# A dense MLP in chunks of 436, 436, 312, 496 and 496 tokens, its pair sums made in place, the pair's norm started beside the third chunk's, and its reciprocal deviation kept in PSUM

## The chip, the cores and the metric

The kernel runs on one core of one Trainium2 chip. The metric is device time of one execution in microseconds (us). The core has a matrix engine (TensorE, PE), a vector engine (VectorE, DVE), an activation engine (ScalarE, ACT), GpSimd (POOL) and a queue engine (SyncE, SP) that issues most DMAs. Each engine runs its own list of instructions in order; semaphores tie the lists together. TensorE writes its products to PSUM, eight banks of 512 fp32 columns; everything else lives in SBUF.

## What is computed

Three layers follow each other: a windowed attention, a gated convolution MLP, and a Fourier mixing with a dense MLP. The change touches the last part alone, with 4 × 544 = 2176 tokens of 512 features:

```python
u = x + mixed
mu = np.mean(u, axis=-1, keepdims=True)
var = np.mean((u - mu) ** 2, axis=-1, keepdims=True)
un = (u - mu) / np.sqrt(var + 1e-06)
ch = np.maximum(un @ w_ch1, 0.0) @ w_ch2     # 512 -> 2048 -> 512
return (u + ch).astype(np.float32)
```

## The kernel before

Features lie on the partitions and tokens along the columns, so a matmul takes a 128 × 128 block of weights and the columns of one chunk of tokens. Each fp32 product is made of three matmuls on high and low parts (`mm3`, L172).

The tokens of the dense MLP are cut into five chunks (`WIDE`, L40). Chunks 0, 1 and 2 go the plain way: `ln(c)` makes the norm in nine steps, `c_g1` (L1002) makes a block of 128 hidden features with 12 matmuls and turns it into a high and a low part `hd` (one ACT and one DVE instruction), and `c_g2` (L1026) adds the block to four accumulators with 12 matmuls. A list of 48 pairs of chunk and block sets the order. In slot v of this list TensorE gets `c_g1(v)` and then `c_g2(v-2)`, 24 matmuls; slots 32 to 47 are those of chunk 2. Blocks alternate between two PSUM banks, so `c_g1(v)` waits until `hd` of block v-2 has been read out of its bank.

Chunks 3 and 4 are a pair: their first layer is made by a scheme of Strassen's kind (`pair`, L1182). Eight rounds q of 7 products, of 6 matmuls each, give four blocks of hidden features; eight plain products would need 48. The second layer is plain, 24 matmuls per round and 192 behind the rounds. Each product lands in one of four banks in turn and is added to sums by DVE (`p1`, `u2`, `w5`, `c21`, `late`). The weights of a round come by DMA: `aw` (L1069) into a buffer of the pool `up`, and two sums of weights `mag` from `sval` in DRAM, which `s_make` (L1052) has computed and stored earlier (slots 17 to 31).

`pair_norm` (L1127) normalises the pair before: per half `x_sum` (L1079), `x_center` (L1093), `x_square` (L1099) and `x_scale` (L1108). A sum over the features is two matmuls with `ones` on a high and low part `sr` (`x_mean`, L1087); they stand in TensorE's list between the slots. Then `t_split` makes the operands of the seven products.

The program fixes the order of TensorE and SP as written; those of DVE, ACT and POOL come from a list scheduler with priorities. `step(lnq)` (L1270) runs one step of the front generator per slot, so `pair_norm`, put into the queue at slot 32, begins when `ln(2)` is through, at slot 36.

The pool `up` has three buffers. Through the last third they hold `cf`, a scratch tile (`cft[0]`), the tokens `uc` of a chunk, and `xsr` and later `aw`:

```python
up = ctx.enter_context(tc.tile_pool(name="up", bufs=3))          # L250
cft.append(up.tile([128, 5, NT], F32, tag="u", name="cf"))       # L957
t = up.tile([128, 3, 512], F32R, tag="u", name="aw")             # L1069
```

Of the kernel before, what the change touches and what calls it, by code (L numbers as in the profile page):

```python
# [12 lines left out]
F32 = mybir.dt.float32  # L13
F32R = mybir.dt.float32r
# [22 lines left out]
KEPT = [0, 16, 1, 17, 2, 18, 3, 19, 4, 5, 6, 7]  # L37
TAIL = [x for m in range(8, 16) for x in (m, 16 + m)]
NT = 436
WIDE = [436, 436, 436, 434, 434]  # L40
NPB, NHB = 3, 3
MT = [(0, 92), (92, 92), (184, 90)]
PLAN = """
# [109 lines left out]
def fused_kernel(ctx: ExitStack, tc: tile.TileContext, d, out):  # L153
# [29 lines left out]
    def f32(ap):  # L183
        return ap.bitcast(F32)
# [750 lines left out]

    ln_t, uc_t, rs_t, cft = {}, {}, {}, []

    def width(c):
        return WIDE[c]

    def load_uc(c, dst=None):
        if dst is None:
            uc_t[c] = up.tile([128, 5, NT], F32, tag="u", name="uc")
            dst = uc_t[c][:, 0:4]
        a0 = a = sum(WIDE[:c])
        z = a0 + width(c)
# [55 lines left out]
    def c_g1(v):  # L1002
        if not 0 <= v < len(plan):
            return
        c, m = plan[v]
        ch, cl = ln_t[c]
        n = width(c)
        o = bank("g1" if m % 2 else "pv")[:, 0:n]
        w = ch1[m]
        for k in range(4):  # L1010
            f = slice(128 * k, 128 * k + 128)
            mm3(o, w[:, 0, f], w[:, 1, f], ch[:, k], cl[:, k], k == 0, k == 3)
        hd = lw.tile([128, 2, NT], F32R, tag="hd", name="hd", bufs=3)[:, :, 0:n]
# [12 lines left out]
    def c_g2(v):  # L1026
        if not 0 <= v < len(plan):
            return
        c, m = plan[v]
        n = width(c)  # L1030
        if m == 0 or c < 2 and m == 8:
            for e in range(4):
                acc[e] = bank(f"a{e}")[:, 0:n]
        for e in range(4):
            c_mm(v, e)
        if m == 15 or c < 2 and m == 7:
            uc = uc_t[c]
            tmp = cft[0][:, 0:4, 0:n]
            for e in range(4):
                dve.tensor_mul(tmp[:, e], acc[e], rs_t[c])  # L1040
            for e in range(4):
                o = uc[:, e, 0:n]
                dve.tensor_add(o, o, tmp[:, e])
                if m == 15:
                    sp.dma_start(out[128 * e:128 * e + 128, NT * c:NT * c + n], o)

    NW = WIDE[3]
    T_SLOTS = []
    T_ORDER = ("b11", "b21", "t2", "t1", "t3", "b22", "t4")
    sval, two, t_hl, s_hl, a_hl = {}, {}, {}, {}, {}  # L1050
# [26 lines left out]
            s_hl[q] = [put(wp, f"w{k}", mags[k]) for k in range(2)]  # L1077

    def x_sum(j):  # L1079
        cf = cft[0]  # L1080
        x, sr = two["x"][j], two["sr"]
        dve.tensor_add(cf[:, 0:2, 0:NW], x[:, 0:2], x[:, 2:4])
        dve.tensor_add(cf[:, 0, 0:NW], cf[:, 0, 0:NW], cf[:, 1, 0:NW])
        act.copy(sr[:, 0], cf[:, 0, 0:NW])
        dve.tensor_sub(sr[:, 1], cf[:, 0, 0:NW], f32(sr[:, 0]))

    def x_mean(o):  # L1087
        sr = two["sr"]
# [8 lines left out]
            dve.tensor_sub(x, x, mu[:, None, :].to_broadcast([128, 2, NW]))  # L1097

    def x_square(j):  # L1099
        cf, sr = cft[0], two["sr"]  # L1100
        for k in (slice(0, 2), slice(2, 4)):
            act.activation(cf[:, k, 0:NW], two["x"][j][:, k], AF.Square)
        dve.tensor_add(cf[:, 0:2, 0:NW], cf[:, 0:2, 0:NW], cf[:, 2:4, 0:NW])
        dve.tensor_add(cf[:, 0, 0:NW], cf[:, 0, 0:NW], cf[:, 1, 0:NW])
        act.copy(sr[:, 0], cf[:, 0, 0:NW])
        dve.tensor_sub(sr[:, 1], cf[:, 0, 0:NW], f32(sr[:, 0]))

    def x_scale(j):  # L1108
        va = x_mean(fbank()[:, 0:NW])
        rs = cft[0][:, 4, 0:NW]  # L1110
        act.activation(rs, va, AF.Sqrt, bias=eps)
        dve.reciprocal(rs, rs)
        for k in (slice(0, 2), slice(2, 4)):
            x = two["x"][j][:, k]
            dve.tensor_mul(x, x, rs[:, None, :].to_broadcast([128, 2, NW]))
# [55 lines left out]
    four = itertools.cycle(("s", "t", "g1", "pv"))  # L1171

    def new_hd():
        return lw.tile([128, 2, NT], F32R, tag="hd", name="hd", bufs=3)[:, :, 0:NW]

    def out_add(c, e, o, a=0, z=NW):
        u = uc_t[c][:, e, a:z]
# [2 lines left out]
        sp.dma_start(out[128 * e:128 * e + 128, t0 + a:t0 + z], u)  # L1180

    def pair():  # L1182
        hbig = [xp.tile([128, 10, NT], F32, tag="x", name="hh") for _ in range(2)]
        block = [hbig[k // 10][:, k % 10, 0:NW] for k in range(20)]
        p1, u2, w5, c21 = block[0:4]
        late = {m: block[4 + k] for k, m in enumerate(x for q in range(8) for x in (q, q + 8))}
        accs = [bank(f"a{e}")[:, 0:NW] for e in range(4)]
        hds = {}

# [12 lines left out]
        for q in range(8):  # L1202
            s_load(q + 1)
            aw, (s24, s13) = a_hl.pop(q), s_hl.pop(q)
            wa = {"a11": aw[:, 0:2, 0:256], "a12": aw[:, 0:2, 256:512], "a22": aw[:, 2].rearrange("p (a b) -> p a b", a=2)}
            for s_, nm in ((s24, "s2 s4"), (s13, "s3 s1")):
                for k, n_ in enumerate(nm.split()):
                    wa[n_] = s_[:, :, 256 * k:256 * k + 256]

            def prod(w, x):  # L1210
                o = bank(next(four))[:, 0:NW]
                for k in range(2):
                    f = slice(128 * k, 128 * k + 128)
                    mm3(o, wa[w][:, 0, f], wa[w][:, 1, f], t_hl[x][k][:, 0], t_hl[x][k][:, 1], k == 0, k == 1)
                return o

            x = prod("a11", "b11")
            with pri("cev"):
                act.copy(p1, x)
            if q:  # L1220
                g2(accs, q - 1, hds.pop(q - 1))
            else:
                c_g2(len(plan) - 1)
            x = prod("s2", "t2")
            with pri("cev"):
# [65 lines left out]
    for u in range(ulast + 1, NM + LAG_G2):  # L1291
# [17 lines left out]
        k = u - (NM - 8)  # L1309
# [9 lines left out]
    for v in range(len(plan)):  # L1319
# [85 lines left out]
```

## Time and profile before

| | us |
|---|---|
| median of 3 runs (lowest, highest) | 779.59 (778.95, 779.71) |
| the profiled execution | 780.79 |
| its span, first to last instruction | 779.0 |
| TensorE busy | 756.3 (97%) |
| VectorE busy | 557.4 (72%) |
| ScalarE busy | 385.9 (50%) |
| mean granted TensorE clock | 0.995 |

The span is shorter than the execution by what lies around the first and the last instruction. A busy TensorE is counted over matmuls that overlap, so the time of a matmul is read from the distance of starts in a full stretch, not from its mean duration. In the chain of waits, the path that ended last, matmuls in a row stand as one piece, and a piece of 12 divided by 12 is that distance.

### The profile page before, as it was taken

Reading aid. Unit: us, or ns where it says so; the run is one execution under the profiler, and the core shown is the slowest. Engines: PE = TensorE matmul, PEld = TensorE weight load, DVE = VectorE, ACT = ScalarE, POOL = GpSimd, SP = SyncE. Lnnn points to the kernel's source line nnn. Section 1 sums busy time; section 2 is a strip of 40 time slices with the busy share of each in tenths; the row PEclk is TensorE's granted clock in tenths of the full one; section 3 lists DMA queues with packets and bytes.
Section 4 is the critical chain, followed back from the end, with each engine's and each line's share of the span. In section 5 each row is a group of like instructions: output and inputs, shape, how many; then the busy total and the mean of one; then the engine's idle time right before and its main releaser. Section 6 shows DMA issues by size and latency. Waiting matters only on the chain.

```text
span 779.0 us, 13835 instructions
## 1 busy us (share of the span) xinstructions
PE 756.3 (97%) x5224; PEld 695.4 (89%) x5224; DVE 557.4 (72%) x1274; ACT 385.9 (50%) x970; POOL 157.7 (20%) x228
## 2 busy tenths in 40 slices
PE   6798999999999999999999999999999999999998
PEld 4587899998989988999898999999999999999997
DVE  5999976778787877799784668876855884545422
ACT  6988767767777766545443265411313421222121
POOL 3755323323223323000223013211100000000000
PEclk9899999999999999999999999999999999999999
DMA  8734301552435333427530492223330124252201
GB/s 312 282 129 177 122 29 76 164 205 73 130 137 178 127 105 117 116 86 252 204 104 0 164 378 84 82 108 121 124 123 0 68 86 137 69 173 76 92 1 46
DMA packets 46594, 98.47 MB, mean 126 GB/s; under 512 B 5224, under 2 KB 26600, under 8 KB 46528
## 3 DMA queue, kind: packets, MB, share of 16 engines
q1 hardware_dynamic: 43504, 86.78, 32.0%
q0 software_dynamic: 3024, 10.81, 4.1%
q8 instruction: 41, 0.67, 0.3%
q14 instruction: 25, 0.20, 0.1%
HBM read 73.98 MB, written 23.59 MB: 125 GB/s over the span
## 4 chain that ended last, share of the span: by engine, by line
PE 81%; DVE 9%; ACT 7%; DMA 2%; issue 1%; POOL 0%; SPq 0%; ACTq 0%
PE ps_a L170 29%; PE ps_g L170 20%; PE ps_pv L170 14%; PE ps_s L170 9%; PE ps_t L170 7%; ACT pb L347 3%; DVE y L562 2%; DVE pb L337 1%; DVE mag L660 1%; DMA raw_w<-in_w_out_dram 1%; DMA raw_w<-in_w_in_dram 1%; DVE w_w L677 1%; DVE mag L665 1%; DVE g L582 1%; ACT h L545 1%
## 5 line engine op out<-in xcount | busy, mean ns | idle before, releaser
L170 PE MATMUL ps_g<-x,w_w 128*128 128x256 f32 (+1 forms) x768 | 112.4, 296 | 2.3 <-DVE w_w L677 1.2
L170 PE MATMUL ps_a<-g,w_w 128*128 128x254 f32 (+1 forms) x768 | 113.5, 295 | 1.1 <-DVE g L582 0.6
L170 PEld LDWEIGHTS ps_g<-x,w_w 128*128 128x128 f32 x768 | 101.2, 190 | 8.9 <-issue 3.1
L170 PEld LDWEIGHTS ps_a<-g,w_w 128*128 128x128 f32 x768 | 101.1, 190 | 5.9 <-issue 3.8
L360 POOL TENSOR_SCALAR pb<-pb,sm 128x224 f32<-128x224 f32 x128 | 85.1, 681 | 81.5 <-DVE sm L355 72.6
L170 PE MATMUL ps_a<-hd,w_w 128*128 128x436 f32 (+1 forms) x384 | 81.6, 361 | 0.0
L562 DVE SCALAR_TENSOR_TENSOR y<-h,convw,y 128x254 f32<-128x254 f32 (+1 forms) x128 | 69.1, 541 | 16.3 <-ACT y L558 15.3
L170 PEld LDWEIGHTS ps_a<-hd,w_w 128*128 128x128 f32 x384 | 72.0, 188 | 4.5 <-DVE hd L1200 0.4
L347 ACT ACTIVATE pb<-pb,sm 128x224 f32<-128x224 f32 x128 | 60.4, 473 | 8.2 <-DVE sm L337 7.9
L192 POOL TENSOR_SCALAR mag<-mag 128x512 f32<-128x512 f32 x32 | 25.6, 800 | 178.8 <-ACT mag L191 178.5
L170 PE MATMUL ps_a<-hd,w_v 128*128 128x436 f32 (+1 forms) x288 | 61.0, 360 | 0.0
L170 PEld LDWEIGHTS ps_a<-hd,w_v 128*128 128x128 f32 x288 | 54.2, 188 | 3.0
L1199 ACT ACTIVATE hd<-hh 128x434 fp32r<-128x434 f32 x32 | 18.1, 568 | 59.5 <-DVE hh L1238 30.8
L170 PE MATMUL ps_s<-qk 64*128 64x224 f32 (+1 forms) x144 | 36.5, 406 | 6.9 <-DMA qk<-in_qk_dram 3.6
L567 ACT ACTIVATE y<-y 128x254 f32<-128x254 f32 (+1 forms) x64 | 27.4, 429 | 29.2 <-DVE y L562 29.1
L1200 DVE SCALAR_TENSOR_TENSOR hd<-hh,hd 128x434 fp32r<-128x434 f32 x32 | 19.4, 609 | 30.4 <-ACT hd L1199 30.4
L170 PE MATMUL ps_t<-qk 64*128 64x224 f32 (+1 forms) x144 | 36.3, 403 | 0.0
L227 ACT CAST w_w<-mag 128x512 fp32r<-128x512 f32 x20 | 12.4, 621 | 47.6 <-PE ps_t L170 11.7
L1015 ACT ACTIVATE hd<-ps_g 128x436 fp32r<-128x436 f32 x24 | 12.8, 533 | 46.5 <-PE ps_g L170 46.5
L582 DVE TENSOR_TENSOR g<-y,g 128x254 fp32r<-128x254 f32 (+1 forms) x64 | 28.5, 445 | 9.6 <-ACT g L580 9.6
L545 ACT ACTIVATE h<-ps_g 128x256 f32<-128x256 f32 (+1 forms) x64 | 25.2, 393 | 20.1 <-PE ps_g L170 20.1
L577 DVE SCALAR_TENSOR_TENSOR y<-y,h 128x254 f32<-128x254 f32 (+1 forms) x64 | 28.3, 442 | 9.5 <-ACT y L567 9.2
(378 smaller groups left out, 1686.2 us busy)
## 6 DMA issues: line engine op xcount, KB each, us to landing
v<-in_v_dram SPq DMA_DIRECT2D x16, 640.0 KB, 5.2
qk<-in_qk_dram SPq DMA_DIRECT2D x16, 464.0 KB, 4.7
raw_r<-in_ch_dram SPq DMA_DIRECT2D x14, 512.0 KB, 5.7
raw_v<-in_ch_dram SPq DMA_DIRECT2D x13, 512.0 KB, 9.0
kept<-w_o SPq DMA_DIRECT2D x12, 512.0 KB, 3.5
w_w<-kept SPq DMA_DIRECT2D x12, 512.0 KB, 4.5
qk<-in_qk_dram SPq DMA_DIRECT2D x16, 304.0 KB, 5.8
u_d<-u SPq DMA_DIRECT2D x4, 1088.0 KB, 5.2
```

Source lines behind the costliest of these rows:

```text
L170: return pe.matmul(o, a, b, start=start, stop=stop)
L192: (clamp or dve).tensor_scalar(mag, mag, TOP, 2.0, op0=ALU.min, op1=ALU.max)
L347: last_exp[0] = act.activation(p, p, AF.Exp, bias=sm[:, k:k + 1], scale=-1.0, accum_out=sm[:, 4 + k:5 + k])
L360: gp.tensor_scalar(pb_of(i, k), pb_of(i, k), sm[:, 12 + k:13 + k], 1.0, op0=ALU.mult, op1=ALU.mult)
L545: act.activation(hbuf[u % NHB][:, h0:h0 + n], h_bank.pop(u), AF.Relu, scale=0.5)
L562: dve.scalar_tensor_tensor(y, o, convw2[:, m, x:x + 1], y, op0=ALU.mult, op1=ALU.add)
L567: act.activation(g_t[u], g_t[u], AF.Tanh, scale=0.5)
L577: dve.scalar_tensor_tensor(y, y, 1.0, hbuf[u % NHB][:, cc:cc + n], op0=ALU.add, op1=ALU.mult)
L582: dve.tensor_sub(gate[u][:, 1], y, f32(gate[u][:, 0]))
L1015: act.activation(hd[:, 0], o, AF.Relu)
L1199: act.activation(hd[:, 0], o, AF.Relu)
L1200: dve.scalar_tensor_tensor(hd[:, 1], o, 0.0, f32(hd[:, 0]), op0=ALU.max, op1=ALU.subtract)
```

## The change

Chunk 2 shrinks from 436 to 312 tokens and chunks 3 and 4 grow from 434 to 496. Tiles whose planes were 436 columns apart are cut anew by `planes`. The pair's sums are made in place: `w5` becomes `late[q]`, `c21` becomes `u2`, and `p1` and `u2` move into the scratch tile `cf`, behind the part that chunk 2's last sums use. Those sums of chunk 2 are made two by two. `pair_norm` gets a queue of its own, so its first step is at slot 32, with one empty step more. The reciprocal deviation `rs` stays in the PSUM bank of the variance. The tokens of chunk 3 are fetched again in round 7 instead of at the end of round 5.

```diff
-WIDE = [436, 436, 436, 434, 434]
+WIDE = [436, 436, 312, 496, 496]
...
+    def planes(t, k, n, at=0):
+        return t.rearrange("p a n -> p (a n)")[:, at:at + k * n].rearrange("p (a n) -> p a n", a=k)
...
-            tmp = cft[0][:, 0:4, 0:n]
-            for e in range(4):
-                dve.tensor_mul(tmp[:, e], acc[e], rs_t[c])
+            tmp = planes(cft[0], 2 if c == 2 else 4, n)
+            k = 2 if c == 2 else 4
+            for e0 in range(0, 4, k):
+                for e in range(e0, e0 + k):
+                    dve.tensor_mul(tmp[:, e % k], acc[e], rs_t[c])
...
     def x_scale(j):
         va = x_mean(fbank()[:, 0:NW])
-        rs = cft[0][:, 4, 0:NW]
+        rs = va
         act.activation(rs, va, AF.Sqrt, bias=eps)
         dve.reciprocal(rs, rs)
...
         yield
         yield
-        two["sr"] = up.tile([128, 5, NT], F32R, tag="u", name="xsr")[:, 0:2, 0:NW]
+        yield
+        two["sr"] = planes(up.tile([128, 5, NT], F32R, tag="u", name="xsr"), 2, NW)
         x_sum(0)
...
-        hbig = [xp.tile([128, 10, NT], F32, tag="x", name="hh") for _ in range(2)]
-        block = [hbig[k // 10][:, k % 10, 0:NW] for k in range(20)]
-        p1, u2, w5, c21 = block[0:4]
+        hbig = [xp.tile([128, 8, NW], F32, tag="x", name="hh") for _ in range(2)]
+        late = {m: hbig[k // 8][:, k % 8] for k, m in enumerate(x for q in range(8) for x in (q, q + 8))}
+        sums = planes(cft[0], 2, NW, 2 * WIDE[2])
+        p1, u2 = sums[:, 0], sums[:, 1]
...
             with pri("cev"):
-                dve.tensor_add(w5, u2, x)
+                dve.tensor_add(late[q], u2, x)
...
             x = prod("a22", "t4")
             with pri("cev"):
-                dve.tensor_add(c21, u2, x)
-            high_low(q + 8, c21)
-            if q in (5, 7):
-                load_uc(3 if q == 5 else 4)
+                dve.tensor_add(u2, u2, x)
+            high_low(q + 8, u2)
+            if q == 7:
+                load_uc(4)
...
-            lnq.append(pair_norm())
+            pairq.append(pair_norm())
...
         step(lnq)
+        step(pairq)
```

The first place is SP's list from the fetch of the pair's tokens `xx` to the weights `aw` of round 1 (`kept_2261`), with the counters that each row waits for (PE, DVE, Activation: what that engine has finished; DMAHW, DMASW: a landed DMA). Before:

```order
L1045 DMA out_dram<-uc 128x436 [waits DVE_49] x2
L950 DMA xx<-u_d_5215 128x4x324 [waits PE_49,Pool_49]
L950 DMA xx<-u_d_5579 128x4x110
L950 DMA xx<-u_d_5579 128x4x434 [waits DMAHW7_49]
L1068 DMA mag_5101<-sval_0_6037 128x512 [waits DMAHW0_49,DMASW7_49,DMASW5_49]
L1068 DMA mag_5102<-sval_1_6039 128x512 [waits DMAHW1_49,DMASW6_49,DMASW4_49]
L1070 DMA aw<-kept_1847 128x1024 [waits DMAHW3_49,DMAHW2_49,DMAHW4_49,DVE_49,PE_49]
L1071 DMA aw<-kept_5662 128x2x256
L1068 DMA mag_5101<-sval_0_6115 128x512 [waits DMAHW0_49,DMASW1_49]
L1068 DMA mag_5102<-sval_1_6117 128x512 [waits DMAHW5_49,DMAHW1_49,DMASW0_49]
L1070 DMA aw<-kept_2261 128x1024 [waits DMAHW6_49,DVE_49,Activation_49]
```

The same place now:

```order
L956 DMA xx<-u_d_5215 128x4x448 [waits DMAHW1_49,PE_49,Pool_49]
L956 DMA xx<-u_d_5579 128x4x48 [waits DMAHW2_49]
L956 DMA xx<-u_d_5579 128x4x496
L1053 DMA out_dram<-uc 128x436 [waits DVE_49] x3
L1053 DMA out_dram<-uc 128x436 [waits DMAHW7_49,DVE_49]
L1075 DMA mag_5101<-sval_0_6037 128x512 [waits DMASW7_49,DMAHW0_49,DMASW5_49,DVE_49]
L1075 DMA mag_5102<-sval_1_6039 128x512 [waits DMAHW1_49,DMASW6_49,DMASW4_49]
L1077 DMA aw<-kept_1847 128x1024 [waits DMAHW5_49,DMAHW4_49,DMAHW6_49,DMAHW2_49,DMAHW7_49,DVE_49,PE_49]
L1078 DMA aw<-kept_5662 128x2x256
L1075 DMA mag_5101<-sval_0_6115 128x512 [waits DMAHW0_49,DMASW1_49]
L1075 DMA mag_5102<-sval_1_6117 128x512 [waits DMAHW1_49,DMASW0_49]
L1077 DMA aw<-kept_2261 128x1024 [waits DMAHW3_49,DMAHW2_49,PE_49]
```

`xx` moved ahead of the stores of chunk 1, and `aw` of round 1 now waits for TensorE and for the two DMAs of `aw` of round 0, where it waited for DVE and ACT.

The second place is ACT's list from the first `sr` of `pair_norm` (`xsr`) to the second one of `x_sum`; `w_w<-mag` are the weight sums of round 0, `hd` the blocks of chunk 2. Before:

```order
L1084 CAST xsr<-cf 128x434 [waits DMAHW3_49,DMAHW2_49,DMAHW4_49,DMAHW1_49,DVE_49]
L1015 ACTIVATE hd<-ps_pv 128x436 [waits PE_49,Activation_49]
L227 CAST w_w_7063<-mag_5101 128x512 [waits DMAHW0_49]
L227 CAST w_w_7066<-mag_5102 128x512 [waits DMAHW1_49]
L1015 ACTIVATE hd<-ps_g_6747 128x436 [waits PE_49,Activation_49]
L1015 ACTIVATE hd<-ps_pv 128x436 [waits PE_49,Activation_49]
L1015 ACTIVATE hd<-ps_g_6808 128x436 [waits DVE_49,PE_49]
L1084 CAST xsr<-cf 128x434 [waits DVE_49,PE_49]
```

Now:

```order
L1091 CAST xsr<-cf 128x496 [waits DMAHW6_49,DMAHW5_49,DMAHW7_49,DMAHW4_49,DVE_49]
L227 CAST w_w_7083<-mag_5101 128x512 [waits DMAHW0_49]
L1021 ACTIVATE hd<-ps_g_6761 128x312 [waits PE_49,Activation_49]
L227 CAST w_w_7086<-mag_5102 128x512 [waits DMAHW1_49]
L1109 ACTIVATE cf<-xx 128x992 [waits DMAHW2_49,DVE_49]
L1091 CAST xsr<-cf 128x496 [waits DVE_49,Activation_49]
```

The casts of the weight sums, which wait for their loads, now stand between the two `sr`, with one block of chunk 2 and a square instead of four blocks.

## Rows read from the trace of the kernel before

**Rows 1.** The page's first part: busy us (share of span) and instructions by engine

```profile
PE 756.3 (97%) x5224; PEld 695.4 (89%) x5224; DVE 557.4 (72%) x1274; ACT 385.9 (50%) x970; POOL 157.7 (20%) x228
```

**Rows 2.** Windows by stage: length, busy us per engine, clock, DMA share, GB/s

```profile
549.37:629.94 80.57, 80.57 (x407) 76.23 (x406) 57.94 (x82) 24.26 (x45) 2.16 (x4) 1.00 0.21 73
642.04:737.48 95.44, 95.44 (x482) 90.60 (x481) 46.61 (x82) 19.54 (x36) 0.00 (x0) 1.00 0.32 106
737.48:770.72 33.24, 33.24 (x169) 31.64 (x169) 9.40 (x16) 7.95 (x14) 0.00 (x0) 1.00 0.07 24
```

**Rows 3.** Chain that ended last, in order of time: start, us, what

```profile
211.39 1.63 PE ps_a L170 x12
213.01 1.42 PE ps_g L170 x12
...
566.56 2.39 PE ps_a L170 x12
...
644.53 1.19 PE ps_s L170 x6
```

**Rows 4.** Timeline of TensorE, shapes of the first two pieces above

```profile
211.14 1.87 PE L170 MATMUL ps_a<-g,w_w 128*128 128x290 f32 x12
212.85 1.58 PE L170 MATMUL ps_g<-x,w_w 128*128 128x256 f32 x12
```

**Rows 5.** Timeline of VectorE, start and us: starts give the distances

```profile
559.26 0.42 DVE L1060 TENSOR_TENSOR mag<-mag 128x256 f32<-128x256 f32 x1
559.60 0.60 DVE L1040 TENSOR_TENSOR cf<-ps_a,uc 128x436 f32<-128x436 f32 x1
...
561.68 1.65 DVE L1043 TENSOR_TENSOR uc<-uc,cf 128x436 f32<-128x436 f32 x3
563.25 0.60 DVE L1016 SCALAR_TENSOR_TENSOR hd<-ps_pv,hd 128x436 fp32r<-128x436 f32 x1
564.89 2.88 DVE L995 RECIPROCAL uc<-uc 128x436 f32<-128x436 f32 x1 [1.04 <-ACT uc L994]
567.69 0.55 DVE L1016 SCALAR_TENSOR_TENSOR hd<-ps_g,hd 128x436 fp32r<-128x436 f32 x1
...
588.45 2.03 DVE L1097 TENSOR_TENSOR xx<-xx,ps_s 128x868 f32<-128x868 f32 x2 [1.60 <-PE ps_s L170]
590.39 0.60 DVE L1085 TENSOR_TENSOR xsr<-cf,xsr 128x434 fp32r<-128x434 f32 x1
```

**Rows 6.** Timeline of ScalarE: a block's relu, two casts, a square

```profile
556.72 0.54 ACT L1015 ACTIVATE hd<-ps_g 128x436 fp32r<-128x436 f32 x1 [4.09 <-PE ps_g L170]
...
572.79 1.22 ACT L227 CAST w_w<-mag 128x512 fp32r<-128x512 f32 x2 [0.77 <-DMA mag<-sval]
...
590.51 0.93 ACT L1102 ACTIVATE cf<-xx 128x868 f32<-128x868 f32 x1 [1.50 <-DVE xx L1097]
```

**Rows 7.** Timeline of POOL: the last store of a weight sum

```profile
559.98 0.54 POOL L1063 DMA_DIRECT2D sval<-mag  x1 [1.29 <-DVE mag L1060]
```

**Rows 8.** DMA issues of the run: tiles, count, size, median us to landing

```profile
sval<-mag POOLq DMA_DIRECT2D x16, 256.0 KB, 2.3
mag<-sval SPq DMA_DIRECT2D x16, 256.0 KB, 3.2
```

**Rows 9.** DMA issues in 612 to 620 us, one fetch of aw alone

```profile
aw<-kept SPq DMA_DIRECT2D x1, 512.0 KB, 3.3
```

**Rows 10.** VectorE by shape, 540 to 779 us: busy us, mean ns

```profile
L1115 DVE TENSOR_TENSOR xx<-xx,cf 128x868 f32<-128x868 f32 x4 | 4.1, 1055 | 0.0
L1097 DVE TENSOR_TENSOR xx<-xx,ps_s 128x868 f32<-128x868 f32 x2 | 2.0, 1055 | 1.6 <-PE ps_s L170 1.6
```

**Rows 11.** Waits of TensorE: us in total, times, longest

```profile
PE ps_s L170 <- DVE smg L440: 1.9, 1, 1.9
PE ps_s L170 <- ACT pgt L489: 1.3, 1, 1.3
```

**Rows 12.** Timeline of TensorE around the first of them

```profile
33.86 0.64 PE L170 MATMUL ps_s<-qk 64*128 64x224 f32 x2 [1.93 <-DVE smg L440]
```

**Rows 13.** Windows behind it, columns as in Rows 2

```profile
34.60:38.00 3.40, 3.40 (x24) 2.49 (x21) 2.99 (x12) 3.37 (x13) 3.22 (x4) 0.50 1.00 407
38.00:41.40 3.40, 3.40 (x18) 3.40 (x17) 2.56 (x5) 1.88 (x7) 0.63 (x2) 0.50 0.53 188
41.40:44.00 2.60, 2.60 (x29) 2.15 (x30) 2.50 (x7) 2.25 (x6) 2.50 (x4) 1.00 0.00 0
```

More of the change, by code (lines that the diff above doesn't have):

```diff
@@ L936, in fused_kernel @@
     ln_t, uc_t, rs_t, cft = {}, {}, {}, []
+    NW = WIDE[3]
     def width(c):
         return WIDE[c]
+    def planes(t, k, n, at=0):
+        return t.rearrange("p a n -> p (a n)")[:, at:at + k * n].rearrange("p (a n) -> p a n", a=k)
     def load_uc(c, dst=None):
         if dst is None:
-            uc_t[c] = up.tile([128, 5, NT], F32, tag="u", name="uc")
+            t = up.tile([128, 5, NT], F32, tag="u", name="uc")
+            uc_t[c] = t if c < 3 else planes(t, 4, NW)
             dst = uc_t[c][:, 0:4]
@@ L1012, in c_g1 @@
             mm3(o, w[:, 0, f], w[:, 1, f], ch[:, k], cl[:, k], k == 0, k == 3)
-        hd = lw.tile([128, 2, NT], F32R, tag="hd", name="hd", bufs=3)[:, :, 0:n]
+        hd = lw.tile([128, 2, NW], F32R, tag="hd", name="hd", bufs=3)[:, :, 0:n]
         with pri("cev"):
@@ L1037, in c_g2 @@
             uc = uc_t[c]
-            tmp = cft[0][:, 0:4, 0:n]
-            for e in range(4):
-                dve.tensor_mul(tmp[:, e], acc[e], rs_t[c])
[L1041 to L1047, printed above, removed]
+            tmp = planes(cft[0], 2 if c == 2 else 4, n)
[3 more added lines that the diff above has]
+                    dve.tensor_mul(tmp[:, e % k], acc[e], rs_t[c])
+                for e in range(e0, e0 + k):
+                    o = uc[:, e, 0:n]
+                    dve.tensor_add(o, o, tmp[:, e % k])
+                    if m == 15:
+                        sp.dma_start(out[128 * e:128 * e + 128, NT * c:NT * c + n], o)
     T_SLOTS = []
@@ L1079, in x_sum @@
     def x_sum(j):
-        cf = cft[0]
+        cf = planes(cft[0], 4, NW)
         x, sr = two["x"][j], two["sr"]
[L1082 to L1085, printed above, removed]
+        dve.tensor_add(cf[:, 0:2], x[:, 0:2], x[:, 2:4])
+        dve.tensor_add(cf[:, 0], cf[:, 0], cf[:, 1])
+        act.copy(sr[:, 0], cf[:, 0])
+        dve.tensor_sub(sr[:, 1], cf[:, 0], f32(sr[:, 0]))
     def x_mean(o):
@@ L1099, in x_square @@
     def x_square(j):
-        cf, sr = cft[0], two["sr"]
+        cf, sr = planes(cft[0], 4, NW), two["sr"]
         for k in (slice(0, 2), slice(2, 4)):
[L1102 to L1106, printed above, removed]
+            act.activation(cf[:, k], two["x"][j][:, k], AF.Square)
+        dve.tensor_add(cf[:, 0:2], cf[:, 0:2], cf[:, 2:4])
+        dve.tensor_add(cf[:, 0], cf[:, 0], cf[:, 1])
+        act.copy(sr[:, 0], cf[:, 0])
+        dve.tensor_sub(sr[:, 1], cf[:, 0], f32(sr[:, 0]))
     def x_scale(j):
         va = x_mean(fbank()[:, 0:NW])
-        rs = cft[0][:, 4, 0:NW]
+        rs = va
         act.activation(rs, va, AF.Sqrt, bias=eps)
@@ L1151, in pair_norm @@
         x_scale(1)
-        cf = cft[0]
-        t1, t2 = cf[:, 0:2, 0:NW], cf[:, 2:4, 0:NW]
+        cf = planes(cft[0], 4, NW)
+        t1, t2 = cf[:, 0:2], cf[:, 2:4]
         dve.tensor_sub(t1, b12, b11)
@@ L1173, in new_hd @@
     def new_hd():
-        return lw.tile([128, 2, NT], F32R, tag="hd", name="hd", bufs=3)[:, :, 0:NW]
+        return lw.tile([128, 2, NW], F32R, tag="hd", name="hd", bufs=3)
     def out_add(c, e, o, a=0, z=NW):
@@ L1182, in pair @@
     def pair():
-        hbig = [xp.tile([128, 10, NT], F32, tag="x", name="hh") for _ in range(2)]
-        block = [hbig[k // 10][:, k % 10, 0:NW] for k in range(20)]
-        p1, u2, w5, c21 = block[0:4]
-        late = {m: block[4 + k] for k, m in enumerate(x for q in range(8) for x in (q, q + 8))}
+        hbig = [xp.tile([128, 8, NW], F32, tag="x", name="hh") for _ in range(2)]
+        late = {m: hbig[k // 8][:, k % 8] for k, m in enumerate(x for q in range(8) for x in (q, q + 8))}
+        sums = planes(cft[0], 2, NW, 2 * WIDE[2])
+        p1, u2 = sums[:, 0], sums[:, 1]
         accs = [bank(f"a{e}")[:, 0:NW] for e in range(4)]
@@ L1226, in pair @@
                 dve.tensor_add(u2, p1, x)
+            if q == 7:
+                load_uc(3)
             x = prod("s1", "t1")
             with pri("cev"):
-                dve.tensor_add(w5, u2, x)
+                dve.tensor_add(late[q], u2, x)
             x = prod("s3", "t3")
             with pri("cev"):
-                dve.tensor_add(late[q + 8], w5, x)
+                dve.tensor_add(late[q + 8], late[q], x)
                 dve.tensor_add(u2, u2, x)
@@ L1241, in pair @@
             with pri("cev"):
-                dve.tensor_add(late[q], w5, x)
+                dve.tensor_add(late[q], late[q], x)
             s_split(q + 1)
@@ L1245, in pair @@
             with pri("cev"):
-                dve.tensor_add(c21, u2, x)
-            high_low(q + 8, c21)
-            if q in (5, 7):
-                load_uc(3 if q == 5 else 4)
+                dve.tensor_add(u2, u2, x)
+            high_low(q + 8, u2)
+            if q == 7:
+                load_uc(4)
         order = [x for q in range(8) for x in (q, q + 8)]
@@ L1267, in fused_kernel @@
     fq = [fft(b) for b in range(4)]
-    lnq = []
+    lnq, pairq = [], []
     def step(queue, name="ln"):
@@ L1359, in fused_kernel @@
     c_g2(len(plan) - 2)
-    while lnq:
-        step(lnq)
+    while pairq:
+        step(pairq)
     pair()
```

## The prediction

> **What bounds the kernel now.** I read the page's first part, then windows by stage, then the chain of waits. TensorE is busy for 97% of the span [rows 1]. From chunk 2's first slot to the last matmuls its busy time equals the length of each window, at full clock [rows 2]: there is no wait to take away there, and all other engines work in TensorE's shadow. So time can be won in this part only by fewer matmul columns, and lost wherever VectorE, ScalarE or a DMA no longer keeps up.
>
> **The columns.** A full stretch gives the distance of two matmuls: 1.42 / 12 = 118 ns at 256 columns, 1.63 / 12 = 136 at 290, 2.39 / 12 = 199 at 436, 1.19 / 6 = 198 at 434 [rows 3, 4], and 33.24 us / 168 = 197.9 at 434 [rows 2]. From 256 to 436 that is 0.44 ns per column and about 6 ns besides, with no floor down to 256, so I take 144 ns at 312 and 225 at 496. Chunk 2 has 16 slots of 24 matmuls: 384 × 124 columns fewer. The pair has 8 × 42 in the products and 2 × 192 in the second layer: 720 × 62 more. 47,616 − 44,640 = 2,976 columns fewer, 2,976 × 0.44 ns = 1.3 us won. The sums with `ones` cancel (4 × 124 columns fewer, 8 × 62 more). The last sum and store at the end have 62 columns more: +0.15 with the store. This is the whole gain; the waits decide.
>
> **The norm in shorter slots.** I set t = 0 at the first matmul of slot 32 (549.4 in the trace of before). Slots 32 and 33 still hold second-layer work of chunk 1: 12 × 144 + 12 × 199 ns = 4.1 us each. The later ones take 24 × 144 ns = 3.45 instead of 4.77. With 0.29 for the variance of chunk 2, the first centring of the pair (slot 37) is reached at 8.2 + 3 × 3.45 + 0.29 = 18.85, where before it had slot 40.
>
> VectorE's distances of starts: 436 columns 1.57 / 3 = 0.52, 256 columns 0.34, 868 columns 1.94 / 2 = 0.97, the reciprocal of 436 columns 2.80 [rows 5]; so some 1.04 ns per column, hence 0.39 at 312, 0.58 at 496, 1.10 at 992, and for reciprocals 2.0 at 312 and 3.2 at 496. From `hd` of slot 33 on, which its relu allows at t = 6.5, VectorE has without a gap: 8 muls and adds of chunk 1's tail (4.2), five instructions of the last `s_make` (2.0), `hd` of slots 33 to 35 (1.2), the first add of `x_sum` (1.1), chunk 2's reciprocal (2.0), the second add (0.6): 11.1, until 17.6. Then `hd` of slot 36, whose matmuls end at 17.1, the cast of `sr` on ScalarE until 18.4, the subtraction until 19.1. TensorE wants it at 18.85: **+0.35** (0 to 0.8).
>
> The second centring (slot 38) is reached at 19.2 + 0.45 + 3.45 = 23.1. Its `sr` follows, on ScalarE, two casts of weight sums, a relu and a square (the order of the change). Those casts wait for `mag`. Its last write is the last `s_make` instruction, at 16.7 in the count above; the store starts 0.3 later [rows 5, 7], lands after 2.3, the load lands after 3.2 [rows 8]: 22.6. Before, ScalarE's wait there was 0.77 and nothing urgent stood behind it [rows 6]. Now the cast (0.53), the late relu (0.35), the second cast (0.53), the square of 992 columns (0.95) and the cast of `sr` (0.6) end at 25.8, VectorE's subtraction at 26.5: TensorE waits until 26.6, **+3.5**. Lower end: if the load were there in time, VectorE's own row of work (add 1.1, two centring subtractions 2.2, add 0.6, then square, cast, subtraction) ends at 24.7, +1.6. Upper end: a load as slow as 4 us, +4.2.
>
> From there VectorE needs until `hd` of slot 42: 2.2 + 2 × 1.7 (squares' adds) + 1.2 (`sr`) + 5 × 0.39 + 2 × 3.2 (reciprocals) + 2.2 (scaling) + 4 × 0.58 (splits) + some 2 of waiting for ScalarE's squares: about 22; TensorE comes to slot 44, which needs that bank, after 0.45 + 6 × 3.45 + 0.9 = 22.05. I take **+0.75** (0 to 1.5). Behind it VectorE has the splits alone and is done before the pair starts. The reciprocals now work in PSUM, which no row shows. The nearest rows: with a PSUM operand a subtraction of 868 columns takes 1055 ns, a product without one 1055 [rows 10]; I take no difference, and 0.4 either way lies within the 0 to 1.5.
>
> [...]
>
> **The weights of round 1.** `cf` now stays in its buffer through the pair, `uc` of chunk 2 holds the second until its stores, so `aw` of round 1 gets the buffer of round 0's. SP's row of it waits for TensorE; round 0 reads `aw` until its last product, and the very next matmul is round 1's first product, on the new `aw`. Nothing can hide this fetch. A fetch alone on the queue lands after 3.3 [rows 9], and some 0.4 pass from the last matmul to the issue and from landing to the first matmul: **+3.7**. Bounds: 3.5, and 5.9 if other transfers lie in its way. Later rounds have two buffers and a whole round (66 × 225 ns = 14.9) for a fetch. The move of chunk 3's tokens to round 7 costs nothing: all of round 7 stands before their use, and the fetch waits for no more than the buffer of round 6. The in-place sums change only what VectorE reads; its rounds are half idle [rows 2] and get no longer than TensorE's.
>
> **The clock.** [...] For the fetch of `aw` I take **+2.9** (0 to 3.4). The wait at the second centring is less sure in its size (1.6 to 4.2), so there I take half as much, **+1.5** (0 to 3.4).
>
> **Sum:** −1.3 + 0.15 + 0.35 + 3.5 + 0.75 + 3.7 + 2.9 + 1.5 = +11.5. The profiled execution took 780.79 and would take 792.3. The median is 1.2 below it, so 791.1 is my forecast for the median.
>
> **Rivals.**
> [...]
> - The norm keeps up: the weight sums land earlier and VectorE is a little ahead, so only the fetch of `aw` and its clock count: −1.3 + 0.15 + 3.7 + 2.9 = +5.45, 785.0. Against: 1.6 us of that wait are VectorE's own work.
> - Not slower: `aw` of round 1 is there in time and the norm keeps up, so only the columns count: −1.15, 778.4. The point from which it decides is whether that fetch can start 3.7 us before round 0's last product; it could with a third free buffer. SP's row speaks against it. The same holds for the thought that the norm beside chunk 2 gains something: no wait stood there [rows 2].
>
> **The numbers.** The forecast (both waits, half clock behind at least one) gets 0.64, its own range 788 to 795; the full clock 0.22; the norm that keeps up 0.10; only columns 0.04. All but the last are above 784; with a clock fall behind both waits in full and a slow fetch it would be 795 or more. Range 784.5 to 795.5. A difference of 0.2%, 1.6 us, is what a measurement of this kernel can tell: slower 0.95, within it 0.03 (the columns alone, −0.15%), faster 0.02.
>
> **What would show it.** In the profile after: pieces of 12 matmuls of 1.73 us in chunk 2 and 2.70 in the pair; a wait of TensorE of 3.5 us on an `xsr` instruction some 23 us into chunk 2, with a ScalarE cast that waits for `mag` ahead of it; a wait of 3.7 us on the DMA of `aw` at round 1's first product; windows at 0.50 behind them. I am wrong if TensorE has no wait on `aw`, if the weight sums land before ScalarE reaches them, or if the full clock holds.

## The result: 1.3% slower

The median went from 779.27 us (777.59 to 779.71, 4 runs) to 788.82 (787.86 to 789.78, 4 runs). The ratio is 1.0131, 95% interval 1.0119 to 1.0144. The forecast was 791.1 with a range of 784.5 to 795.5.

### The profile page after: what moved, and what is told of

It is laid out like the page before. It is cut to its first block, busy times and chain, and to the rows that moved or that the text cites. A ratio compares the mean times of both kernels' runs of the same rounds, so it can differ in the third digit from the quotient of the medians.

```text
span 786.7 us, 13855 instructions
## 1 busy us (share of the span) xinstructions
PE 756.2 (96%) x5224; PEld 677.3 (86%) x5224; DVE 561.1 (71%) x1274; ACT 386.5 (49%) x970; POOL 158.5 (20%) x228
## 4 chain that ended last, share of the span: by engine, by line
PE 67%; DVE 12%; issue 9%; ACT 7%; DMA 2%; POOL 1%; SPq 0%; POOLq 0%; ACTq 0%; DVEq 0%
PE ps_a L170 22%; PE ps_g L170 16%; PE ps_pv L170 10%; PE ps_s L170 9%; PE ps_t L170 7%; ACT pb L347 3%; DVE y L562 1%; DVE mag L660 1%; POOL sval L1070 1%; DVE pb L337 1%; DMA raw_w<-in_w_out_dram 1%; DVE w_w L677 1%; DVE mag L665 1%; DMA qk<-in_qk_dram 1%; ACT h L545 1%
## 5 line engine op out<-in xcount | busy, mean ns | idle before, releaser
L170 PE MATMUL ps_a<-hd,w_w 128*128 128x436 f32 (+2 forms) x384 | 81.0, 359 | 1.5 <-DVE cf L1048 1.5
L170 PEld LDWEIGHTS ps_a<-hd,w_w 128*128 128x128 f32 x384 | 69.4, 191 | 8.3 <-DVE cf L1048 1.6
L170 PE MATMUL ps_a<-hd,w_v 128*128 128x436 f32 (+2 forms) x288 | 59.0, 353 | 0.0
L170 PEld LDWEIGHTS ps_a<-hd,w_v 128*128 128x128 f32 x288 | 51.1, 188 | 4.3
L558 ACT ACTIVATE y<-h,convw 128x254 f32<-128x254 f32 (+1 forms) x64 | 33.5, 524 | 2.1 <-DVE g L582 1.5
L170 PEld LDWEIGHTS ps_pv<-pt,v 128*64 128x64 f32 x480 | 27.1, 141 | 8.6 <-issue 6.4
L170 PE MATMUL ps_pv<-pt,v 128*64 128x128 f32 x480 | 34.5, 287 | 0.0
```

The costliest lines, as they stand in the source:

```text
L170: return pe.matmul(o, a, b, start=start, stop=stop)
L558: act.mul(y, hb[:, cc:cc + n], convw2[:, m, 1:2])
```

## The profile after

The profiled execution took 788.46 us, its span 786.7; before, 780.79 and 779.0. Slot 32 of chunk 2 starts at 547.58 in it and at 549.37 before. These 1.8 us lie ahead of everything that the change touches (the wait for the first `qk` was 1.3 us here, 2.9 before), so I compare from slot 32 to the end of the last matmul: 235.39 us (547.58 to 782.97) against 226.08 (549.37 to 775.45), +9.3, and the end behind it grew from 3.55 to 3.73. That is the +9.5 of the medians.

The page's first part answers [rows 1]; TensorE's busy time is the same, the weight loads' is not.

```profile
PE 756.2 (96%) x5224; PEld 677.3 (86%) x5224; DVE 561.1 (71%) x1274; ACT 386.5 (49%) x970; POOL 158.5 (20%) x228
```

The windows of the new kernel, to be held against [rows 2]: length, busy us by engine, granted clock, DMA share, GB/s.

```profile
547.58:613.83 66.25, 61.79 (x407) 59.70 (x406) 54.78 (x76) 23.00 (x43) 2.17 (x4) 1.00 0.25 87
628.58:634.25 5.67, 5.67 (x18) 4.65 (x19) 0.00 (x0) 0.57 (x1) 0.00 (x0) 0.70 0.90 296
634.25:739.53 105.28, 105.28 (x469) 87.80 (x468) 50.20 (x80) 20.08 (x34) 0.00 (x0) 1.00 0.27 87
739.53:782.97 43.44, 43.44 (x193) 35.88 (x191) 12.55 (x20) 8.66 (x14) 0.00 (x0) 1.00 0.09 33
```

Chunk 2 is no longer filled: 61.79 us busy in 66.25. From round 1 to the end TensorE is busy throughout again, but for 18 matmuls at a mean granted clock of 0.70. TensorE's waits behind slot 32 (us in total, times, longest), where the list of before has none, answering [rows 11]:

```profile
PE ps_pv L170 <- DMA aw<-kept: 3.4, 1, 3.4
PE ps_t L170 <- DVE xsr L1092: 2.4, 1, 2.4
PE ps_a L170 <- DVE cf L1048: 1.5, 3, 0.7
PE ps_s L170 <- DVE xsr L1092: 0.5, 1, 0.5
```

And TensorE's timeline at these places, which answers [rows 3, 4] (start, us, piece, in brackets the idle time before it):

```profile
555.77 1.87 PE L170 MATMUL ps_pv<-chl,w_w 128*128 128x312 f32 x12
558.06 0.66 PE L170 MATMUL ps_a<-hd,w_w 128*128 128x312 f32 x3 [0.41 <-DVE cf L1048]
559.42 1.22 PE L170 MATMUL ps_a<-hd,w_w 128*128 128x312 f32 x6 [0.70 <-DVE cf L1048]
560.98 0.70 PE L170 MATMUL ps_a<-hd,w_w 128*128 128x312 f32 x3 [0.34 <-DVE cf L1048]
...
569.32 0.72 PE L170 MATMUL ps_s<-xsr,ones 128*128 128x496 f32 x2 [0.45 <-DVE xsr L1092]
...
575.91 0.69 PE L170 MATMUL ps_t<-xsr,ones 128*128 128x496 f32 x2 [2.43 <-DVE xsr L1092]
576.44 1.88 PE L170 MATMUL ps_pv<-chl,w_w 128*128 128x312 f32 x12
...
624.37 0.83 PE L170 MATMUL ps_g<-t_r,aw 128*128 128x496 f32 x3
628.58 1.65 PE L170 MATMUL ps_pv<-t_w,aw 128*128 128x496 f32 x6 [3.38 <-DMA aw<-kept]
630.02 4.39 PE L170 MATMUL ps_a<-hd,w_w 128*128 128x496 f32 x12
634.25 1.50 PE L170 MATMUL ps_s<-t_w,w_w 128*128 128x496 f32 x6
```

A wait costs more than its brackets show (at the second centring 2.7 instead of 2.43). I price each by the distance of starts less the matmuls between (0.143 us at 312 columns, 0.225 at 496). Accumulators of slot 34 (ready by 557.49, second layer through at 561.52): 2.3. First centring 0.8, second 2.7. The bank of slot 44 cost 0.4. `aw` 3.5. The twelve at 630.02 take 4.23 to the next start instead of 2.70, and with 0.1 in the six before them the half clock (granted 0.50 from 629.97 to 633.38) cost 1.6. Behind the second centring the twelve at 576.44 take 1.72, with 1.00 granted from 575.91 to 579.89.

The wait on `cf` was not foreseen. It begins on VectorE (first two rows) and at the DMA issues between 545 and 549 us (tile, count, KB, median us to landing):

```profile
549.95 0.48 DVE L1022 SCALAR_TENSOR_TENSOR hd<-ps_pv,hd 128x312 fp32r<-128x312 f32 x1 [1.13 <-ACT hd L1021]
556.31 0.69 DVE L1062 TENSOR_TENSOR mag<-w_r 128x512 f32<-128x512 f32 x1 [5.87 <-DMA sval<-mag]
```

```profile
xx<-u_d SPq DMA_DIRECT2D x1, 992.0 KB, 9.5
xx<-u_d SPq DMA_DIRECT2D x1, 896.0 KB, 5.1
sval<-mag POOLq DMA_DIRECT2D x1, 256.0 KB, 8.1
xx<-u_d SPq DMA_DIRECT2D x1, 96.0 KB, 4.8
```

The first instruction of the last `s_make` overwrites `mag`, whose store took 8.1 us instead of the 2.3 of [rows 8]. The fetch of `xx`, now issued at 545.42, was under way; before the change it was issued at 563.79, behind all these stores. VectorE took its instructions in the order of its list: that one started at 556.31, the tail of chunk 1 (L1048), which stands behind it and frees the accumulators, at 557.31. The store (issued at 548.20) is seen landed at 556.3, just behind the 992 KB fetch (issued at 546.66, landed at 556.1); from 548 to 549 us the DMAs moved 409 GB/s. How the fetch delays the store is not shown: in e2_paced below, two stores issued beside the same fetch are seen landed after 5.6 and 6.1 us, ahead of its last part (8.7).

## The experiments

All edits are to the changed kernel; each ratio is to runs of the kernel before on the same chip. `hold(a, b)` makes the DMA `a` wait for the end of `b`; `held` keeps such instructions.

**e1_aw_free: does keeping `cf` cause the wait on `aw`?**

```diff
-        sums = planes(cft[0], 2, NW, 2 * WIDE[2])
-        p1, u2 = sums[:, 0], sums[:, 1]
+        p1, u2 = late[7], late[15]
...
         for q in range(8):
+            if q == 7:
+                sums = planes(up.tile([128, 5, NT], F32, tag="u", name="sums"), 2, NW)
+                p1, u2 = sums[:, 0], sums[:, 1]
```

> The change, but with the two running sums of rounds 0 to 6 in the blocks of late[7] and late[15], which are free until round 7, and in a buffer of their own in round 7; cf's buffer is then free for the weights aw of round 1, as before the change. Theory: in the changed kernel's trace the wait on aw takes 3.5 us of TensorE's time and the half clock right behind it 1.6, both because cf is kept: no wait on aw in round 1, full clock through the pair, 788.8 - 5.1 = 783.7. Rival 1: the half clock is owed to the earlier waits in chunk 2 and only comes late; then it stays, 785.3. Rival 2: the fetch of aw is late for a reason of its own, whatever the buffer: 788.8.

784.15 us, ratio 1.0071 (1.0052 to 1.0090). TensorE's timeline:

```profile
575.86 0.69 PE L170 MATMUL ps_t<-xsr,ones 128*128 128x496 f32 x2 [2.49 <-DVE xsr L1092]
576.38 2.70 PE L170 MATMUL ps_pv<-chl,w_w 128*128 128x312 f32 x12
578.88 2.63 PE L170 MATMUL ps_a<-hd,w_w 128*128 128x312 f32 x12
...
625.45 0.83 PE L170 MATMUL ps_g<-t_r,aw 128*128 128x496 f32 x3
626.11 1.51 PE L170 MATMUL ps_pv<-t_w,aw 128*128 128x496 f32 x6
627.46 2.86 PE L170 MATMUL ps_a<-hd,w_w 128*128 128x496 f32 x12
```

The wait on `aw` and the slow pieces behind it are gone, so kept `cf` causes both. But this time the second centring's wait, 2.49 us, left a half clock (24 matmuls in 4.97 us instead of 3.44, with 0.69 granted from 575.86 to 581.35): that is the fall which the prediction had put at +1.5 and which the changed kernel's own profile does not have.

**e6_fill: is the half clock the price of standing still?**

```diff
+            if q == 1:
+                o = bank("pv")[:, 0:NW]
+                for k in range(15):
+                    mm(o, ones, t_hl["t4"][0][:, 0], k == 0, k == 14)
             x = prod("a11", "b11")
```

> The change, with 15 extra matmuls of 496 columns (15 x 225 ns = 3.4 us, into a PSUM bank that the next product overwrites) ahead of round 1's first product: TensorE works while it would wait for aw, the fetch of which is as late as before. [...]

787.12 us, ratio 1.0119 (1.0099 to 1.0139). If the standstill makes the half clock behind `aw`, its 1.6 us come back here: 788.8 − 1.6 = 787.2. The times alone do not part it from the changed kernel; the timeline does:

```profile
624.71 3.56 PE L170 MATMUL ps_pv<-t_v,ones 128*128 128x496 f32 x15
628.57 1.60 PE L170 MATMUL ps_pv<-t_w,aw 128*128 128x496 f32 x6 [0.29 <-DMA aw<-kept]
630.00 2.85 PE L170 MATMUL ps_a<-hd,w_w 128*128 128x496 f32 x12
632.70 1.52 PE L170 MATMUL ps_s<-t_w,w_w 128*128 128x496 f32 x6
```

`aw` is as late as ever, and the twelve behind it take 2.70 instead of 4.23; the mean granted clock of this execution is 1.000, the changed kernel's 0.996. So the half clock there comes from the standstill.

**e4_old_widths: the change without the new widths** (and `hd` with its 436 columns again).

```diff
-WIDE = [436, 436, 312, 496, 496]
+WIDE = [436, 436, 436, 434, 434]
...
```

> The change with the old widths (436, 436, 436, 434, 434): norm beside chunk 2's, sums in place, cf kept, reciprocals in PSUM, but slots of 4.77 us instead of 3.43. Theory: the wait on aw and its half clock do not hang on the widths (+5.1), the waits in chunk 2 do: in slots that are a third longer VectorE keeps up: 779.3 + 5.1 = 784.4. Rival 1: the fetch of xx runs ahead of the stores of the weight sums here too and VectorE's stall of 5.9 us makes TensorE wait for cf and for xsr as in the changed kernel: 786.7 or more. Rival 2: the widths themselves (columns) are the loss and the rest is free: 779.3.

783.16 us, ratio 1.0063 (1.0048 to 1.0078). No wait in chunk 2 is left on its list, though the norm stands beside chunk 2's here too; the wait on `aw` is (3.4), with a longer half clock (18 matmuls in 6.41 us instead of 3.56, with 0.52 granted):

```profile
640.59 2.51 PE L170 MATMUL ps_pv<-t_w,aw 128*128 128x434 f32 x6 [3.43 <-DMA aw<-kept]
...
647.00 1.35 PE L170 MATMUL ps_s<-t_w,w_w 128*128 128x434 f32 x6
```

So of the change's 9.5 us the kept `cf` makes about 5 (by the times; in this trace the stretch from slot 32 on is 6.2 longer than before, by the longer half clock), and the short slots the rest.

**e2_paced: the fetch of `xx` held behind two stores.** The first transfer of `xx` waits for the stores of `s_make(6)`.

```diff
+            ld = sp.dma_start(dst[:, :, a - a0:a - a0 + n], u_d[b][:, :, o:o + n])
+            if c > 2 and held and a == WIDE[0] * 2 + WIDE[2] and "xx" not in held:
+                held["xx"] = 1
+                for k in range(2):
+                    hold(ld, held[6, k])
...
```

> The change, but the fetch of the pair's tokens xx waits until the two stores of the weight sums of s_make(6) have landed. Theory: that fetch (2 MB) ran ahead of those stores and made them land after 7 us instead of 2.3, VectorE stood idle 5.87 us on it with the tail of chunk 1 behind, and TensorE waited for the accumulators of slot 34 (2.3 us in all by the distances of the matmuls): VectorE's wait on the store falls to some 1 us, TensorE's wait on cf is gone (-2.3), the first centring's too (-0.8), and the second's falls from 2.7 to the 1.6 or less that is VectorE's own work (0 to -1.1): 784.6 to 785.7. Rival: the wait on cf is VectorE's own queue, with s_make's last instructions ahead of the tail; it stays, and the tokens that now land later add up to 1: 788.8 to 789.8.

790.16 us, ratio 1.0154 (1.0137 to 1.0171): no gain where 3 to 4 us were expected, though the part on the stores came true. The list of TensorE's waits has nothing on `cf` and nothing at the first centring any more:

```profile
PE ps_pv L170 <- DMA aw<-kept: 3.5, 1, 3.5
PE ps_t L170 <- DVE xsr L1104: 2.5, 1, 2.5
PE ps_t L170 <- DVE xsr L1125: 1.4, 1, 1.4
```

What went came back. The second centring still waits 2.5, now with a half clock behind it (1.5: 24 matmuls in 4.97 us instead of 3.44), and a variance is 1.4 late, as VectorE's 3.27 us reciprocal stands ahead of an add of 0.66 that the variance needs. The reason is in the starts: from the first centring's sum to the second's it is 6.59 us here (567.15 to 573.74) and 6.59 in the changed kernel (569.32 to 575.91). That much VectorE and ScalarE need between the two; one slot gives 4.0. Here the weight sums have landed before the first of them (at 566.2), so their load is in time, and the wait is no shorter: VectorE now takes the two subtractions behind their casts ahead of the centring (L1116).

```profile
566.36 0.68 DVE L228 TENSOR_TENSOR w_w<-mag,w_w 128x512 fp32r<-128x512 f32 x1
...
568.45 0.68 DVE L228 TENSOR_TENSOR w_w<-mag,w_w 128x512 fp32r<-128x512 f32 x1
569.05 2.27 DVE L1116 TENSOR_TENSOR xx<-xx,ps_s 128x992 f32<-128x992 f32 x2
```

**e3_mag_late: ScalarE's casts of the weight sums out of the way.** The load of round 0's `mag` waits for the last square root.

```diff
+                ld = sp.dma_start(mags[k], sval[q, k])
+                if q == 0:
+                    hold(ld, held["x1"])
...
```

> The change, but the load of the weight sums of round 0 into mag waits for the square root of the pair's second half, so that ScalarE's two casts of them no longer stand ahead of the cast of sr of the second centring. Theory of the prediction: the casts and their wait for mag (3.6 us of ScalarE idle) hold the second centring; without them VectorE's own work leaves 1.6 of its 2.7 us at most: -1.1 to -2.7, 786.1 to 787.7. Rival: VectorE, late from the tail of chunk 1, sets that wait alone: 788.8, and the wait on xsr stays at 2.4. The wait on cf stays at 1.5 and that on aw at 3.4 by both.

787.98 us, ratio 1.0126 (1.0108 to 1.0144), which shows no difference from the changed kernel. In its timeline the second centring's wait fell from 2.43 to 1.61 and the variance's 1.37 took its place:

```profile
573.78 0.69 PE L170 MATMUL ps_t<-xsr,ones 128*128 128x496 f32 x2 [1.61 <-DVE xsr L1102]
...
590.05 0.69 PE L170 MATMUL ps_t<-xsr,ones 128*128 128x496 f32 x2 [1.37 <-DVE xsr L1123]
```

The casts, with VectorE's two subtractions behind them (L228), make 0.8 of that wait; the rest is VectorE's own row.

**e8_slot: one more slot between the two centrings.**

```diff
         x_center(0)
         x_sum(1)
         yield
+        yield
```

> The change, with one more slot of chunk 2 (3.43 us) between the pair's two centrings; all that follows in the norm comes a slot later. Theory: the second centring waits because one slot is less than what VectorE and ScalarE have to do between the two (two centring subtractions 2.2, adds 1.2 and 0.7, cast 0.6, subtraction 0.7, evictions of a slot 0.4 and the two splits of weight sums 1.3: 7.1 us): with two slots (6.9) the 2.7 us go to 0.2 or less, and the end of the norm has room: 786.1 to 786.5; the waits on cf (2.3) and on aw stay. Rival: VectorE has no room later either, and the wait comes back at the variances, at slot 44's bank or at t2: 788.8.

786.42 us, ratio 1.0104 (1.0089 to 1.0120): by the ratios 2.1 us less than the change, near the theory. The second centring's sum starts at 576.59, 7.44 after the first, without a wait. But the variance's 1.4 appears here too, as the rival said, and in the trace the stretch from slot 32 on is only 1.3 shorter than the changed kernel's (234.14 against 235.39).

**e5_norm_after: the norm behind chunk 2's again** (`lnq` instead of `pairq`).

> The change, but the pair's norm again behind chunk 2's norm in the same queue instead of beside it. The fetch of xx then stands behind the last stores of the weight sums, as before the change, and the two centrings come some slots later. Theory: the waits on cf (2.3 us) and on xsr at the centrings (0.8 + 2.7) and the 0.4 at slot 44 are the price of having the norm beside chunk 2's: they go (-6.2), and as the second scaling then stands in slot 46, the parts of t2 come some 3 us after the pair's second product wants them (+3.2), with up to 1.6 of half clock behind it, and the variance of the second half is 1.4 late as in the two runs before: 787.2 to 788.8. So short slots cost about the same either way. Rival: the norm has time enough behind chunk 2's too, and only aw is left: 788.8 - 6.2 = 782.6.

789.06 us, ratio 1.0147 (1.0119 to 1.0175). All waits at centrings and on `cf` are gone; what comes instead:

```profile
PE ps_pv L170 <- DMA aw<-kept: 3.9, 1, 3.9
PE ps_t L170 <- DVE t_w L1131: 3.1, 1, 3.1
PE ps_t L170 <- DVE xsr L1113: 1.4, 1, 1.4
```

TensorE reaches the pair's second product 3.1 us before the parts of `t2` are there, and a half clock follows (1.65: 17 matmuls in 5.48 us instead of 3.83). So with slots of 3.43 us this place behind chunk 2's norm is too late, and beside it the norm collides.

**e7_best, e9_best, e11_best: all remedies.** e7 is e1, e2, e3 and e8 together and one more slot ahead of the second scaling; the load of round 0's weights stands at slot 45 instead of 44, behind the square root that it waits for.

> The change with all remedies: sums of rounds 0 to 6 in free blocks (aw of round 1 gets cf's buffer), the fetch of xx held behind the stores of s_make(6), the load of round 0's weight sums held behind the last square root, one more slot between the two centrings and one more ahead of the second scaling. Theory: every wait that the change brought is gone, and what is left of it is the columns (-1.6 by the trace's own distances) and the longer last sums (+0.2): 779.3 - 1.4 = 777.9, a ratio of 0.998. Rival: with slots of 3.43 us VectorE can't keep up in chunk 2, whatever the order, and some 2 us or more of waits come up elsewhere (variances, t2, the pair's start): 780 or more, a ratio of 1.001 or more.

784.42 us, ratio 1.0082 (1.0066 to 1.0098). Chunk 2 is free of waits (546.91 to 607.11, 60.2 us), but `aw` waits again, 3.76 us: chunk 2's tail uses `cf` last, the norm's end has moved towards it, and the third buffer was handed out otherwise. A half clock that costs 2.8 us stands behind it (0.56 granted over 18 matmuls). In e9 that tail has blocks of its own:

```diff
-            tmp = planes(cft[0], 2 if c == 2 else 4, n)
+            tmp = spare[0][:, :, 0:n] if c == 2 else planes(cft[0], 4, n)
...
+        spare.append(hbig[1][:, 4:6])
```

> The kernel e7_best, but the tail of chunk 2 takes its products in the blocks of late[6] and late[14] instead of cf, so that the fetch of round 1's aw waits for nothing later than the splits of t1 and t2. In e7_best every wait of chunk 2 was gone (from slot 32 to the pair's first product 60.2 us where 60.1 is the matmuls alone), and only the wait on aw had come back (3.8 us, and some 2.8 of half clock behind it), since aw of round 1 had again been given round 0's buffer. Theory: that was all; 784.4 - 6.6 = 777.8, against 778.0 to 779.3 of the kernel before a ratio of 0.998 (columns -1.6, end +0.2). Rival: without the wait VectorE or a later fetch makes TensorE wait in the pair; 780 or more.

779.10 us, ratio 1.0006 (0.9992 to 1.0019): the 5 us are back. Two waits were left, 1.1 us on `xsr` and 0.7 on `hd`. e11 moves three places for them:

```diff
         x_sum(0)
+        yield
...
-        x_scale(0)
+        va = x_mean(fbank()[:, 0:NW])
         x_square(1)
+        x_scale(0, va)
...
-        yield
         x_scale(1)
```

> The kernel e9_best with three places moved: one slot more ahead of the first centring (there TensorE still waited 1.1 us, since the cast of sr waits for chunk 1's stores to leave the buffer that xsr takes), no extra slot ahead of the second scaling, and the second half's squares ahead of the first half's reciprocal. Theory: of the two waits left in e9_best (1.3 us at the first centring, 0.9 at a relu of the pair's round 0) the first goes and the second shrinks or stays: 1.3 to 2.2 us less than e9_best, a ratio to the kernel before of 0.998 to 0.999: the columns' 1.6 us and nothing else. Rival: VectorE's row is as long as ever and the wait comes up at a variance or in round 0: 1.000 to 1.002.

777.91 us against 778.56, ratio 0.9992 (0.9982 to 1.0002). Its windows of chunk 2 and the pair:

```profile
546.87:607.06 60.19, 60.19 (x407) 59.64 (x406) 49.94 (x68) 22.17 (x41) 2.17 (x4) 1.00 0.29 97
607.06:772.03 164.97, 164.71 (x734) 136.58 (x732) 77.99 (x126) 33.91 (x58) 0.00 (x0) 1.00 0.24 79
```

225.16 us where the kernel before has 226.08: so 0.9 us is what the widths are worth in this one trace with no listed wait left in the stretch (two gaps of 0.3 and 0.4 us by distances remain in round 1); by the times it can't be told from no change.

**e10_old_free: e4 and e1 together.**

> The change with the old widths (as in e4) and with the sums of rounds 0 to 6 in free blocks (as in e1): norm beside chunk 2's, sums in place, reciprocals in PSUM, slots of 4.77 us. Theory: with these widths the wait on aw with its half clock was the only loss, so this equals the kernel before: a ratio of 1.000, within 0.2%; norm beside, sums in place and PSUM cost and give nothing in themselves. Rival: one of them costs something that the waits hid, 1.002 or more.

779.80 us, ratio 1.0023 (1.0007 to 1.0038). In its trace the same stretch takes 226.03, as before the change, with no wait. That execution (780.55) is long ahead of it: slot 32 starts at 549.19, where e4 with the same widths has 545.76. Whether all of the 0.2% of the times lies there (the runs scatter from 777.58 to 784.83) is left open.

## Why the prediction was right

| Step | forecast, us | trace or run, us |
|---|---|---|
| columns | -1.3 | -1.6 (e11_best, without its two gaps) |
| end | +0.15 | +0.2 |
| accumulators of slot 34 | none | **+2.3** |
| first centring | +0.35 | +0.8 |
| second centring | +3.5 | +2.7 |
| bank of slot 44 | +0.75 | +0.4 |
| `aw` of round 1 | +3.7 | +3.5 |
| half clock behind `aw` | +2.9 | +1.6 |
| half clock behind the centring | +1.5 | 0 |

The forecast column gives 11.5. The other gives 9.9 for the 9.5 measured; prices by distances are no more exact here.

**`aw`.** Right in place, cause and size: e1 takes it away, e4 keeps it without the widths.

**The second centring.** Right in place, in part in cause. On ScalarE the order was the one forecast, in the changed kernel:

```profile
572.18 0.62 ACT L227 CAST w_w<-mag 128x512 fp32r<-128x512 f32 x1 [3.62 <-DMA mag<-sval]
572.70 0.43 ACT L1021 ACTIVATE hd<-ps_g 128x312 fp32r<-128x312 f32 x1
573.03 0.61 ACT L227 CAST w_w<-mag 128x512 fp32r<-128x512 f32 x1
573.54 1.03 ACT L1109 ACTIVATE cf<-xx 128x992 f32<-128x992 f32 x1
574.47 0.59 ACT L1091 CAST xsr<-cf 128x496 fp32r<-128x496 f32 x1
```

The weight sums land at t = 24.6 (forecast 22.6), TensorE comes 2.6 us later than reckoned, from the unforeseen wait, and so the wait is shorter. But the late load, to which the forecast gave 1.9 of its 3.5, is not what decides: e2 had it in time and still waited 2.53, where the forecast's lower end for that case was 1.6. That lower end left the two subtractions of the weight sums (L228) out of VectorE's row. Only e3, which takes them and the casts away, comes to 1.61. The forecast's own terms also add up to some 3.2, not 3.5.

**The step that failed** is the sentence that VectorE works "without a gap" from slot 33 on. It put no wait for the store of `mag` there, and took the store at the 2.3 us of [rows 8], a median over a run in which `xx` was fetched behind these stores. I had followed where the fetch went on SP's queue, not what it would run ahead of. VectorE stood still for 5.87 us, and TensorE lost 2.3 at the accumulators, a term that the sum doesn't have; e2, with the stores ahead of the fetch, has no such wait. That this nearly makes up for the clock terms, which were 2.8 too high, is luck.

**The clock.** The kind was right, the size not. The forecast's 2.9 behind `aw` and 1.5 behind the second centring were estimates of mine; no run of this kernel shows them, and its trace has 1.6 and 0 in their place. Behind `aw` the granted clock was 0.50 for 3.41 us, half as long as in [rows 13]; in other runs the low stretch behind a wait cost 1.4 to 2.9. Behind the second centring e1 and e2 show 1.5 each.

**PSUM.** "No difference" holds. The reciprocal of 434 columns in the kernel before (in SBUF), then in e4_old_widths (in PSUM):

```profile
604.20 2.87 DVE L1112 RECIPROCAL cf<-cf 128x434 f32<-128x434 f32 x1 [2.26 <-ACT cf L1111]
```

```profile
586.21 2.88 DVE L1119 RECIPROCAL ps_s<-ps_s 128x434 f32<-128x434 f32 x1 [2.23 <-ACT ps_s L1118]
```

The two differ by some 10 ns.

**The rivals.** The full clock (the forecast without its two clock terms, 786.7) fell with the 0.70 granted over round 1's first 18 matmuls, "the norm keeps up" (785.0) with the rows above. "Columns only" (778.4) is not the changed kernel; e11_best, which makes its condition true (an early fetch of `aw` and a norm in time), agrees with it, but its interval holds no change at all too.

## What to carry to other kernels

When a large transfer is moved earlier, list the small transfers that it now runs ahead of, and who waits for them in order. In a stage where the matmul engine is full, shorter slots shorten every deadline of the work beside it: compare what the other engines need between two of its steps (6.6 us here) with what the slots give (4.0), before counting columns. A buffer that is kept longer is paid at the first tile that would have used it.

## What the runs showed of the hardware

- A 256 KB store landed after 2.3 us alone, and after 8.1 and 7.7 when issued behind 2 MB of fetches in the changed kernel. In e2 two stores ahead of these fetches landed after 2.3 and 2.5, two issued beside them after 5.6 and 6.1.
- TensorE's granted clock after the waits in chunk 2 and the pair: no fall after 1.61 (e3), 2.43 (the changed kernel) and 2.58 us (e6); half clock after 2.49 (e1) and 2.53 (e2), and after all eight waits of 3.1 to 3.9 (over the 18 matmuls behind `aw` 0.70 granted in the changed kernel and e8, 0.52 in e4, 0.56 in e7). So around 2.5 us the length of a wait alone does not tell which of the two follows. What a fall cost lay between 1.4 and 2.9 us.
